# Reordering VectorE within a period of fused attention: reciprocal and output copy

## The chip, the cores and the metric

One core of one Trainium2 chip. The metric is the device time of one execution in microseconds (us); the median of several runs counts.

## The reference

Attention with a learned position bias, then two dense two-layer networks one after the other, all in float32.

```python
scores = scale * np.matmul(q, k.transpose(0, 1, 3, 2))      # B, H, S, D = 4, 8, 576, 64
...
scores = scores + bias.transpose(2, 0, 1)[None, :, :, :]
scores = scores - np.max(scores, axis=-1, keepdims=True)
attn = np.exp(scores)
attn = attn / (np.sum(attn, axis=-1, keepdims=True) + 1e-09)
x = np.matmul(attn, v)             # to (2304, 512)
h = x @ w_in;  x = (h - np.tanh(h)) @ w_out                 # d_ff = 2048
h = x @ w_in2; r = np.maximum(h, 0); x = (s * r * r + b) @ w_out2
```

The bias is a small network over log distances, computed once.

## The kernel before

The kernel has three stages: the bias table, attention, and the dense layers. Every engine carries out its instructions in the order in which the program issues them; the order is written out by hand (`manual_schedule`), and nothing rearranges it. Semaphores between engines follow from the tiles.

Attention is a software pipeline over 80 periods: 16 pairs (two heads of one batch entry) times 5 row tiles t. Tiles 0 to 3 hold 128 rows for each of two heads, so two score tiles (j = 0, 1); tile 4 holds the last 64 rows of both heads in one score tile. A row tile x = n passes through the engines over several turns n of the loop `for n in range(NK + 6)`:

- turn x: TensorE computes scores into `s` (`emit_score`, L382; two buffers); VectorE adds the bias, once for each j, and finds the extreme of each row (`emit_bias`, L389).
- turn x + 1: ScalarE takes the exponential with row sums (`emit_exp`, L403), GpSimd adds a small constant to the sums (`emit_sum`, L407), VectorE inverts them (`emit_inverse`, L411).
- turn x + 2: GpSimd scales the rows into `pn` (`emit_norm`, L420).
- turn x + 3: TensorE transposes `pn` into two banks `t0` and `t1` (`emit_transpose`, L426), and sometimes short tails into `c`; ScalarE copies `t0`, VectorE copies `t1` into `pt` (`emit_parts`, L464, or L466 and L467 for tile 4). Each of these banks exists once.
- later turns: products with v into the bank `o` (`emit_pv`, L481). A pair has two units, u = 0 with 256 rows (tiles 0 and 1) and u = 1 with 320 rows (tiles 2 to 4). Unit 0 of pair i is multiplied in turns 5i + 5 to 5i + 7, unit 1 in turns 5i + 8 and 5i + 9. `o` exists once. When a unit is complete, VectorE copies it into `xo` and SP stores that to memory (`emit_out`, L488 and L489).

So VectorE's queue in one turn n holds: bias additions of n (two, or one for tile 4), the reciprocal of n - 1, the copy of `t1` for n - 3, in two of five turns the output copy, and in every fourth turn from 15 on a tick of the weights (`weights_tick`). A tick turns packed weights into float32 with three VectorE instructions (L130, L139, L142), two on ScalarE (L122, L138) and a subtraction on GpSimd (L87). TensorE's queue in a turn: scores of n, transposes of n - 3, products. GpSimd's: scaling of n - 2, sums of n - 1, then the subtraction of a tick. SP issues in program order the loads of q and k (`load_qk`, L158), of v (L164), of bias tiles (`load_bias`, L177, inside `emit_bias`), of weights (`fetch`, L111), and the stores of `xo`.

The dense layers follow (`gemm1` L312, `gemm2` L569); TensorE works through them without the attention's buffers, and the first products of the first layer are already issued in the last turns of attention.

Of the kernel before, what the change touches and what calls it, by code (L numbers as in the profile page):

```python
# [58 lines left out]
def tile_kernel(ctx, tc, qk, vd, wcat, wts, sb, ltab, psib, ipsi8, out):  # L59
# [110 lines left out]
    def load_bias(hp, k):  # L170
        e, t = ORDER[k]
        if (hp, k) not in bias_t:
            bias_t[hp, k] = bp.tile([128, S], F32, tag="bias", name="bias")
        bt = bias_t[hp, k]
        i0, n = IT[t]
        for r, ee in enumerate((e,) if e < 2 else (0, 1)):
            nc.sync.dma_start(out=bt[r * 64:r * 64 + n], in_=bass.AP(  # L177
                tensor=bias_d.tensor, offset=bias_d.offset + i0 // 4 * (32 * PITCH - 4) + 4 * (2 * hp + ee) * PITCH + 15,
                ap=[[32 * PITCH - 4, n // 4], [PITCH - 1, 4], [1, S]]))
# [156 lines left out]
    with ExitStack() as ca:  # L336
# [30 lines left out]
        def heads_of(x):  # L367

            t = periods[x][1]
            return [(0, 8, 2)] if t == 4 else [(0, 2 * t, 0), (1, 2 * t + 1, 1)]  # L370

        def emit_score(x):
            i, t = periods[x]
            q, kk = qk_t[i]
            for j, _, e in heads_of(x):
                s = s_t[x, j] = ps_s.tile([128, 2, 512], F32, tag="s", name="s")
                for ee in ((e,) if e < 2 else (0, 1)):
                    o = s if e < 2 else s[ee * 64:ee * 64 + 64]
                    n = IT[t][1]
                    for c in range(2):  # L380
                        h = slice(c * 64, c * 64 + 64)
                        nc.tensor.matmul(o[0:n, c, 0:288], q[h, ee, t * 128:t * 128 + n], kk[h, ee], start=True, stop=True)  # L382

        def emit_bias(x):
            i, t = periods[x]
            for j, k, _ in heads_of(x):
                raw = sp.tile([128, S], F32, tag="raw", name="raw", bufs=3)
                mn = sp.tile([128, 1], F32, tag="mn", name="mn", bufs=3)
                nc.vector.tensor_tensor_reduce(  # L389
                    out=raw.rearrange("p (c j) -> p c j", c=2), in0=s_t.pop((x, j))[:, :, 0:288],  # L390
                    in1=bias_t[pairs[i][0], k].rearrange("p (c j) -> p c j", c=2),
                    scale=-0.125, scalar=3.0e38, op0=ALU.add, op1=ALU.min, accum_out=mn)
                raw_t[x, j] = (raw, mn)

                if i >= 2 and bq and 36 - len(bq) < 11 + i // B * 9 + (max(0, k + 1) if i % B == B - 1 else 0):
                    load_bias(*bq.pop(0))

        def emit_exp(x):
            sm = sums[x] = sp.tile([128, 2], F32, tag="sm", name="sm", bufs=4)
            for j, _, _ in heads_of(x):  # L400
                raw, mn = raw_t.pop((x, j))
                p = p_t[x, j] = pp.tile([128, S], F32, tag="p", name="p")
                nc.scalar.activation(out=p, in_=raw, func=AF.Exp, scale=-1.0, bias=mn, accum_out=sm[:, j:j + 1])  # L403

        def emit_sum(x):
            sm = sums[x][:, 0:len(heads_of(x))]
            nc.gpsimd.tensor_scalar(out=sm, in0=sm, scalar1=1.0, scalar2=1e-9, op0=ALU.mult, op1=ALU.add)  # L407

        def emit_inverse(x):
            sm = sums[x][:, 0:len(heads_of(x))]  # L410
            nc.vector.reciprocal(sm, sm)  # L411

        def emit_norm(x):

            pn = n_t[x] = np_.tile([128, 9 * 128], F32, tag="pn", name="pn")
            sm = sums.pop(x)
            for j, _, e in heads_of(x):
                p = p_t.pop((x, j))
                for a, b, c in ([(0, S, 0), (448, 512, S)], [(0, S, 0)], [(0, 512, 640), (512, S, S)])[(e + 1) % 3]:
                    nc.gpsimd.tensor_scalar(out=pn[:, c:c + b - a], in0=p[:, a:b], scalar1=sm[:, j:j + 1],  # L420
                                            scalar2=0.0, op0=ALU.mult, op1=ALU.add)
# [12 lines left out]
        def emit_transpose(x):  # L434
            i, t = periods[x]
            if t in (1, 3):
                emit_tails(0, x - 1)
            pn = n_t[x]
            ab = tr_t[x] = [ps_t.tile([128, 8, 64], F32, tag=f"t{r}", name=f"t{r}") for r in range(2)]
            for j in range(8 if t < 4 else 5):  # L440
                for r in range(2):
                    if t < 4:
                        c = j * 128 + j // 4 * 128
                    else:
                        c = j * 128 if j < 4 else (512, 448)[r]
                    turned(r, ab[r][:, j], pn[ROWS[r], c:c + 128])
            if t in (2, 4):
                emit_tails(1, x - 2)
                del n_t[x - 2], n_t[x - 1]
            if t == 4:  # L450
                del n_t[x]

        def emit_parts(x):

            i, t = periods[x]
            u = int(t > 1)
            if (i, u) not in unit_t:
                unit_t[i, u] = gp_.tile([128, 9, 320], F32, tag="pt", name="pt")
            pt = unit_t[i, u]
            ab = tr_t.pop(x)  # L460
            for r, copy in ((0, nc.scalar.copy), (1, nc.vector.tensor_copy)):
                if t < 4:
                    c0 = t % 2 * 128 + r * 64
                    copy(pt[:, 0:8, c0:c0 + 64], ab[r])  # L464
                else:
                    copy(pt[:, 4 * r:4 * r + 4, 256:320], ab[r][:, 0:4])  # L466
                    copy(pt[ROWS[r], 8, 256:320], ab[r][ROWS[r], 4])  # L467
            if t in (2, 4):
                done = unit_t[i, int(t == 4)]
                nc.scalar.copy(done[:, 8, 0:256], tr_t.pop("c").rearrange("p k r q -> p (k r q)"))  # L470

        def emit_pv(i, u, j):

            r0, n = UNITS[u]
            v = v_t[i]
            if j == 0:
                o_t[i, u] = ps_o.tile([128, 512], F32, tag="o", name="o")[:, 0:n]
            o = o_t[i, u]
            for e in range(2):
                h = slice(e * 64, e * 64 + 64)  # L480
                nc.tensor.matmul(o[h], v[:, e, j], unit_t[i, u][:, 8 if j == 4 else 4 * e + j, 0:n], start=(j == 0), stop=(j == 4))  # L481

        def emit_out(i, u):
            hp, b = pairs[i]
            r0, n = UNITS[u]
            del unit_t[i, u]
            xo = sp.tile([128, 320], F32, tag="xo", name="xo", bufs=2)[:, 0:n]
            nc.vector.tensor_copy(xo, o_t.pop((i, u)))  # L488
            nc.sync.dma_start(out=x1_d[hp][:, b * S + r0:b * S + r0 + n], in_=xo)  # L489

        PV = {}
        for i in range(len(pairs)):
            for u, (m, parts) in enumerate(((5 * i + 5, (2, 2, 1)), (5 * i + 8, (2, 3)))):
                js = list(range(5))
                for c, k in enumerate(parts):
                    PV.setdefault(m + c, []).append((i, u, js[:k]))
                    js = js[k:]  # L500
        for n in range(NK + 6):
            def now(lag):
                return 0 <= n - lag < NK

            if n == NK:
                s_ctx.close()
                hpool.append(h_ctx.enter_context(tc.tile_pool(name="ps_h", bufs=4, space=PSUM, side="right", reuse_waits="tile")))
            if now(2):
                emit_norm(n - 2)
            if now(0):  # L510
                emit_score(n)
            if now(1):
                emit_exp(n - 1)
                emit_sum(n - 1)
            if now(0):
                emit_bias(n)
            if now(1):
                emit_inverse(n - 1)
            if now(3):
                emit_transpose(n - 3)  # L520
                emit_parts(n - 3)
            for i, u, js in PV.pop(n, []):
                for j in js:
                    emit_pv(i, u, j)
                if js[-1] == 4:
                    emit_out(i, u)
            if n in FT:
                fetch(FT[n])
            for f in work.pop(n, []):
                f()  # L530
            for _ in range(TICKS.get(n, 0)):
                weights_tick()
            for f in PRE.get(n, []):
                f()
        assert not PV
        assert not work
# [143 lines left out]
```

## Time and profile before

| | |
|---|---|
| median of three runs | 1091.99 us (1091.46 to 1092.54) |
| the profiled execution | 1091.09 us |
| its span, first to last instruction | 1089.3 us |
| TensorE, matrix products | 1065.3 us busy (98%) |
| VectorE | 642.6 us (59%) |
| ScalarE | 469.6 us (43%) |
| GpSimd | 327.5 us (30%) |
| mean granted TensorE clock | 0.998 |

A busy share is a mean over stages with different limits. In the profile PE is TensorE, PEld its weight loads, DVE is VectorE, ACT ScalarE, POOL GpSimd, SP the queue that issues most transfers. Matrix products are pipelined, so the ends in their records are modelled.

### The profile page before, as it was taken

What the parts mean: (1) busy time and instruction counts of PE and PEld (TensorE: products, weight loads), DVE (VectorE), ACT (ScalarE), POOL (GpSimd) and SP (SyncE); (2) the same over time, 40 slices, a digit from 0 to 9 for tenths busy, and PEclk for the clock granted to TensorE, in tenths of its full rate; (3) what the DMA queues carried; (4) which work ended last, traced back from release to release, by engine and by line L of the source; (5) the groups of instructions that cost most, each with busy time, mean ns of one, the idle gap of its engine ahead of it and who ended that gap; (6) DMA issues with size and microseconds to landing.
All of it is one profiled execution on the core that took longest, in us unless ns stands there. A gap on an engine that the chain in (4) does not pass through costs nothing.

```text
span 1089.3 us, 18185 instructions
## 1 busy us (share of the span) xinstructions
PE 1065.3 (98%) x7000; PEld 838.0 (77%) x7000; DVE 642.6 (59%) x1223; ACT 469.6 (43%) x955; POOL 327.5 (30%) x454
## 2 busy tenths in 40 slices
PE   9999999999999999999999999999999999999998
PEld 6566555555678888899888888888888888888897
DVE  8878889778679832232322499997343343343344
ACT  8977677677545422222222354553222222222222
POOL 0066777678625510020300046344030030010000
PEclk9999999999999999999999999999999999999999
DMA  7957555253181010020100365500100020010010
GB/s 283 314 191 257 189 180 183 85 180 113 42 318 65 10 59 1 0 79 1 58 1 1 135 218 206 193 1 20 58 20 1 4 75 1 1 58 1 1 39 20
DMA packets 41334, 99.65 MB, mean 91 GB/s; under 512 B 5024, under 2 KB 11552, under 8 KB 41248
## 3 DMA queue, kind: packets, MB, share of 16 engines
q1 hardware_dynamic: 40960, 98.24, 26.1%
q8 instruction: 55, 0.90, 0.3%
q10 hardware_dynamic: 288, 0.26, 0.1%
q14 instruction: 31, 0.25, 0.1%
HBM read 73.41 MB, written 25.07 MB: 90 GB/s over the span
## 4 chain that ended last, share of the span: by engine, by line
PE 83%; POOL 4%; DVE 3%; DMA 2%; issue 2%; ACT 1%; ACTq 0%; SPq 0%; DVEq 0%; POOLq 0%
PE h L312 36%; PE a L569 36%; PE o L481 5%; PE s L382 4%; POOL pn L420 3%; PE t L426 2%; DMA qk<-in_qk 1%; DVE raw L389 1%; POOL w L87 1%; DVE pt L464 1%; DMA vv<-in_vd 1%; PE c L426 0%; POOL sm L407 0%; DVE wx L142 0%; DVE wx L130 0%
## 5 line engine op out<-in xcount | busy, mean ns | idle before, releaser
L312 PE MATMUL h<-x,w 128*128 128x512 f32 (+1 forms) x1920 | 420.6, 368 | 0.0
L312 PEld LDWEIGHTS h<-x,w 128*128 128x128 f32 x1920 | 337.4, 188 | 62.4 <-issue 1.3
L569 PE MATMUL a<-ring,w 128*128 128x512 f32 (+1 forms) x960 | 210.2, 368 | 0.0
L569 PE MATMUL a<-w,ring 128*128 128x512 f32 x864 | 208.9, 389 | 0.0
L569 PEld LDWEIGHTS a<-ring,w 128*128 128x128 f32 x960 | 168.3, 189 | 30.0
L569 PEld LDWEIGHTS a<-w,ring 128*128 128x128 f32 x864 | 161.1, 188 | 32.8
L87 POOL TENSOR_TENSOR w<-wx,w 128x512 fp32r<-128x512 f32 x64 | 96.0, 1500 | 209.7 <-ACT w L122 196.4
L333 DVE TENSOR_TENSOR ring<-ring 128x512 fp32r<-128x512 f32 (+1 forms) x160 | 110.3, 690 | 78.5 <-ACT ring L332 78.5
L332 ACT CAST ring<-ring 128x512 fp32r<-128x512 f32 (+1 forms) x160 | 92.3, 577 | 135.7 <-DVE ring L327 96.6
L420 POOL TENSOR_SCALAR pn<-p,sm 128x576 f32<-128x576 f32 (+2 forms) x224 | 136.8, 627 | 36.1 <-DVE sm L411 30.5
L326 DVE TENSOR_TENSOR ring<-ring 128x512 f32<-128x512 f32 (+1 forms) x80 | 53.0, 662 | 149.9 <-ACT ring L325 149.9
L323 DVE TENSOR_TENSOR ring<-h,ring 128x512 f32<-128x512 f32 (+1 forms) x80 | 50.8, 635 | 141.0 <-ACT ring L322 140.7
L84 POOL TENSOR_SCALAR x<-xr 128x512 fp32r<-128x512 f32 (+1 forms) x36 | 25.9, 719 | 330.1 <-DMA xr<-x_d 330.1
L403 ACT ACTIVATE p<-raw,mn 128x576 f32<-128x576 f32 x144 | 110.7, 773 | 13.8 <-DVE mn L389 13.0
L325 ACT ACTIVATE ring<-h 128x512 f32<-128x512 f32 (+1 forms) x80 | 44.4, 555 | 165.7 <-PE h L312 165.7
L322 ACT ACTIVATE ring<-h 128x512 f32<-128x512 f32 (+1 forms) x80 | 44.3, 554 | 164.6 <-PE h L312 164.6
L389 DVE CUSTOM_DVE_ANT_0 raw<-s,bias 128x576 f32<-128x576 f32 x144 | 103.7, 752 | 18.5 <-PE s L382 14.6
L382 PE MATMUL s<-qk 64*128 64x288 f32 (+1 forms) x640 | 93.8, 433 | 11.5 <-DVE mn L389 11.1
L481 PE MATMUL o<-pt,vv 128*64 128x256 f32 (+1 forms) x640 | 96.0, 422 | 0.0
L382 PEld LDWEIGHTS s<-qk 64*128 64x128 f32 (+1 forms) x640 | 46.3, 175 | 55.7 <-DVE mn L389 24.4
L426 PEld LDWEIGHTS t<-ident,pn 64*128 64x128 f32 x1184 | 52.5, 140 | 16.8 <-DVE pt L464 6.0
L122 ACT CAST w<-wx 128x512 fp32r<-128x512 f32 x64 | 39.7, 621 | 58.8 <-DVE wx L142 57.7
(49 smaller groups left out, 841.0 us busy)
## 6 DMA issues: line engine op xcount, KB each, us to landing
w<-in_wts SPq DMA_DIRECT2D x64, 512.0 KB, 4.7
qk<-in_qk SPq DMA_DIRECT2D x16, 864.0 KB, 6.6
bias_d<-m SPq DMA_DIRECT2D x36, 296.0 KB, 4.4
bias<-bias_d SPq DMA_DIRECT2D x32, 288.0 KB, 4.7
xr<-x_d SPq DMA_DIRECT2D x28, 256.0 KB, 3.0
vv<-in_vd SPq DMA_DIRECT2D x16, 320.0 KB, 4.2
x_d<-o SPq DMA_DIRECT2D x16, 256.0 KB, 2.1
out_x<-o SPq DMA_DIRECT2D x16, 256.0 KB, 2.1
```

The lines of the kernel that those rows point to most:

```text
L87: nc.gpsimd.tensor_tensor(out=lo, in0=raw, in1=hi.bitcast(F32), op=ALU.subtract)
L312: nc.tensor.matmul(h, a, x, start=(k == 0), stop=(k == 3 * KD - 1))
L326: nc.vector.tensor_tensor(out=g, in0=t, in1=t, op=ALU.mult)
L332: nc.scalar.copy(gh, g)
L333: nc.vector.tensor_tensor(out=gl, in0=g, in1=gh.bitcast(F32), op=ALU.subtract)
L382: nc.tensor.matmul(o[0:n, c, 0:288], q[h, ee, t * 128:t * 128 + n], kk[h, ee], start=True, stop=True)
L389: nc.vector.tensor_tensor_reduce(out=raw.rearrange("p (c j) -> p c j", c=2), in0=s_t.pop((x, j))[:, :, 0:288], in1=bias_t[pairs[i][0], k]. ...
L403: nc.scalar.activation(out=p, in_=raw, func=AF.Exp, scale=-1.0, bias=mn, accum_out=sm[:, j:j + 1])
L420: nc.gpsimd.tensor_scalar(out=pn[:, c:c + b - a], in0=p[:, a:b], scalar1=sm[:, j:j + 1], scalar2=0.0, op0=ALU.mult, op1=ALU.add)
L426: nc.tensor.transpose(out_, in_, ident[ROWS[r], ROWS[r]])
L481: nc.tensor.matmul(o[h], v[:, e, j], unit_t[i, u][:, 8 if j == 4 else 4 * e + j, 0:n], start=(j == 0), stop=(j == 4))
L569: nc.tensor.matmul(o, x, y, start=first and j == 0, stop=last and j == 2)
```

## The change

In a turn, the reciprocal of n - 1 is issued behind the copy of the transposed bank instead of in front of it. An output copy that became due in a turn is put on a list, and is issued in the next turn by `emit_bias`, in front of its last bias addition (so between the two additions of a turn with two). Its store moves along with it. From turn 79 on the output copies are issued at the end of their own turn, as before.

```diff
         def emit_bias(x):
             i, t = periods[x]
             for j, k, _ in heads_of(x):
+                if j == len(heads_of(x)) - 1:
+                    emit_outs()
                 raw = sp.tile([128, S], F32, tag="raw", name="raw", bufs=3)
...
+        outs = []
+
+        def emit_outs():
+            while outs:
+                emit_out(*outs.pop())
+
...
             if now(0):
                 emit_bias(n)
-            if now(1):
-                emit_inverse(n - 1)
             if now(3):
                 emit_transpose(n - 3)
                 emit_parts(n - 3)
+            if now(1):
+                emit_inverse(n - 1)
             for i, u, js in PV.pop(n, []):
                 for j in js:
                     emit_pv(i, u, j)
                 if js[-1] == 4:
-                    emit_out(i, u)
+                    outs.append((i, u))
+            if not now(-1):
+                emit_outs()
```

## Rows read from the trace of the kernel before

**Rows 1.** Busy time by stretch: start:end, length, busy (instructions) by engine, granted clock, DMA.

```profile
340.00:366.00 26.00, 26.00 (x117) 21.52 (x116) 26.00 (x30) 12.68 (x24) 18.46 (x14) 1.00 0.07 21
...
192.00:195.00 3.00, 2.82 (x23) 1.81 (x25) 1.55 (x5) 1.88 (x5) 2.55 (x6) 0.50 0.00 0
```

**Rows 2.** Waits, 48 to 300 us: who waited for whom, total us, times, longest.

```profile
DVE sm L411 <- POOL sm L407: 18.5, 30, 1.6
...
PE t L426 <- DVE pt L464: 3.7, 8, 1.0
...
PE t L426 <- DVE pt L467: 2.5, 5, 0.9
```

**Rows 3.** Timeline, TensorE then VectorE, an undisturbed turn: start, us, engine, line, operation.

```profile
72.09 1.24 PE L382 MATMUL s<-qk 64*128 64x288 f32 x8
...
73.88 1.08 PE L481 MATMUL o<-pt,vv 128*64 128x256 f32 x8
...
72.21 0.49 DVE L488 COPY xo<-o 128x320 f32<-128x320 f32 x1 [0.66 <-PE o L481]
72.90 0.76 DVE L389 CUSTOM_DVE_ANT_0 raw<-s,bias 128x576 f32<-128x576 f32 x1 [0.20 <-PE s L382]
```

**Rows 4.** Timeline, TensorE then VectorE, a tick behind a 256-wide unit.

```profile
122.94 1.24 PE L382 MATMUL s<-qk 64*128 64x288 f32 x8
...
124.61 1.30 PE L481 MATMUL o<-pt,vv 128*64 128x320 f32 x8
127.64 0.72 PE L382 MATMUL s<-qk 64*64 64x288 f32 x8 [1.73 <-DVE mn L389]
...
129.62 1.84 PE L481 MATMUL o<-pt,vv 128*64 128x320 f32 x12
...
123.67 0.42 DVE L488 COPY xo<-o 128x256 f32<-128x256 f32 x1
...
126.83 0.74 DVE L389 CUSTOM_DVE_ANT_0 raw<-s,bias 128x576 f32<-128x576 f32 x1
```

**Rows 5.** Timeline, TensorE then VectorE, a tick behind a 320-wide unit.

```profile
164.35 1.08 PE L481 MATMUL o<-pt,vv 128*64 128x256 f32 x8
166.04 1.43 PE L382 MATMUL s<-qk 64*128 64x288 f32 x8 [0.61 <-DVE mn L389]
...
161.47 0.17 DVE L411 RECIPROCAL sm<-sm 128x2 f32<-128x2 f32 x1 [0.53 <-POOL sm L407]
...
163.09 0.83 DVE L130 SCALAR_TENSOR_TENSOR wx<-wx,wsg 128x512 int32<-128x512 int32 x1
...
165.24 0.74 DVE L389 CUSTOM_DVE_ANT_0 raw<-s,bias 128x576 f32<-128x576 f32 x1
```

**Rows 6.** Timeline of VectorE, a tick in the turn after a 320-wide unit.

```profile
150.35 0.68 DVE L130 SCALAR_TENSOR_TENSOR wx<-wx,wsg 128x512 int32<-128x512 int32 x1
150.95 1.51 DVE L139 TENSOR_SCALAR wsg<-w 128x512 int32<-128x512 int32 x1
...
152.98 0.75 DVE L389 CUSTOM_DVE_ANT_0 raw<-s,bias 128x576 f32<-128x576 f32 x1
```

**Rows 7.** Timeline, TensorE then VectorE, a turn in which TensorE waits for a bank copy.

```profile
142.50 0.68 PE L426 MATMUL t<-ident,pn 64*128 64x64 f32 x15 [0.46 <-DVE pt L467]
143.12 1.30 PE L481 MATMUL o<-pt,vv 128*64 128x320 f32 x8
...
141.71 0.40 DVE L466 COPY pt<-t 128x256 f32<-128x256 f32 x1
```

**Rows 8.** Timeline of TensorE, the first turns of attention.

```profile
57.23 0.71 PE L426 MATMUL t<-ident,pn 64*128 64x64 f32 x15 [0.97 <-DVE pt L464]
...
59.26 0.71 PE L426 MATMUL t<-ident,pn 64*128 64x64 f32 x15 [0.30 <-DVE pt L464]
```

**Rows 9.** Timeline of TensorE, the products after a wait that ends at 190.84 us.

```profile
190.84 0.72 PE L382 MATMUL s<-qk 64*64 64x288 f32 x8 [1.73 <-DVE mn L389]
...
193.23 2.83 PE L481 MATMUL o<-pt,vv 128*64 128x320 f32 x12
```

## The prediction

> **What bounds the kernel now.** I read the stretches first [rows 1]: between 340 and 366 us, in the two dense layers, TensorE has no gap, and that lasts from about 291 us to the end. So whatever the attention stage (48 to 291 us) loses or gains arrives whole at the end, and only TensorE's position at the end of attention counts. In attention it has gaps, 1.73 us at one place [rows 4]. There every fourth period carries a piece of weight unpacking (a "tick": three VectorE instructions, 2.2 to 2.8 us).
>
> The table of waits comes next [rows 2]. VectorE stands 18.5 us, in 30 places, in front of the reciprocal (its sum comes from GpSimd). Behind it in VectorE's queue stands the copy of the transposed bank, and for that copy TensorE waits 3.7 and 2.5 us. These 6.2 us are what the first half of the change can reach. No row of TensorE waiting for an output copy is in that table: today each one is done before TensorE comes back to its bank.
>
> Last the timeline around the output copies, to see how narrow that is. In an undisturbed period [rows 3] scores start at 72.09, the first bias addition at 72.90 (0.81 behind them), and the first product of the next unit at 73.88 (1.79 behind them). The output copy runs at 72.21, before the addition, in time in which VectorE waits for scores anyway.
>
> **The change part by part.** *Reciprocal behind the copy.* No instruction more or less. Where the sum is ready, the copy starts 0.08 earlier (consecutive VectorE instructions overlap by 0.08, [rows 6]: 0.68 long, next start 0.60 later) and the reciprocal about 0.6 later. Behind the reciprocal waits the normalisation on GpSimd; its tile is transposed two periods later, so I put this at nothing: the two periods of other TensorE work hide it. If that cover were gone it would cost up to 0.6 in a period. Where the sum is late, the copy no longer waits, and TensorE gains what it waited.
>
> *Output copy between the additions.* The copies in front of the last periods stay put; 29 of 32 move, with their DMA issues. On SP's queue the DMA now follows the next period's first bias load and the q/k, v and weight fetches of its own period: these go earlier, the store goes later, and its first reader comes periods later. Nothing. On VectorE the copy (0.42 or 0.49) leaves idle time and stands in front of the second addition; score and exponent have that much slack in an undisturbed period. On TensorE it is different. There is one o bank. The next unit's first product, at the end of the same period, must wait for the copy; the copy must wait for the first addition, and that for this period's scores. Counted from the start of the scores: addition at 0.81, 0.68 for it, the copy 0.49, 0.07 to TensorE ([rows 4]: the addition at 126.83 ends at 127.57, the score starts at 127.64). That is 2.05, where TensorE is ready at 1.79 [rows 3]: 0.26 late. For the 256-wide unit, 0.81 + 0.68 + 0.42 + 0.07 = 1.98 against 1.67 ([rows 4], 122.94 to 124.61): 0.31 late. TensorE is in order, so the next scores are late too.
>
> The Trainium skill (Perfetto Trace Analysis, Matmuls) advises rotating product groups through banks, so that emptying one overlaps filling the next, and so speaks against moving this copy back with one bank. The trace of before shows no such wait, the copy coming in time; by the rule it would be exposed, which gives the places below, and without it their price is that of the first rival.
>
> The 29 places, as estimates from the same views:
>
> - Undisturbed: six at 0.26 and four at 0.31, 2.8 us.
> - A tick behind the end of a 256-wide unit (two, [rows 4]). Today copy, tick, addition; TensorE does its products at 124.61 and waits 1.73 for the addition. Then the tick starts at 123.67 and, 2.82 long (126.83 less 123.67 and 0.34), ends at 126.49; the addition takes 0.68, the copy ends at 127.59, the products start at 127.66, three us late, and the next scores 1.22 behind (1.30 less the overlap), at about 128.9 against 127.64. The wait on the bank copy behind them (about 0.5 from start to start) falls away: 0.7 each, 1.4 us.
> - A tick in the period that now holds the copy (three, [rows 6]). The copy adds 0.41 to a queue TensorE already waits for: 1.2 us.
> - A tick behind a 320-wide unit (two, [rows 5]). VectorE no longer waits for sum (0.53) or products: bank copy from 160.94 (0.59 to the next start), reciprocal (0.08), tick from 161.60. The tick took 2.15 there (163.09 to 165.24), 2.63 where it follows the bank copy directly [rows 6]. I take 2.63, being the order that it will have: addition at 164.23, output copy to 165.40, products at 165.47, next scores at about 166.49 against 166.04: 0.45 each, 0.9 us. With 2.15 it would be nothing.
> - Where TensorE waits on a bank copy today (twelve places with their neighbours, [rows 7] is one). There the copies start at 141.18 instead of 141.71, the addition at 141.85, the output copy ends at 142.95, the products start at 143.02 against 143.12. The wait goes, but lateness of the output copy takes all but 0.1 of it. So four times -0.1, twice -0.2 for a pair of places where a tick has made VectorE late, twice +0.1, and -0.2 and -0.4 at single places: -1.2 us.
> - The start [rows 8]: no output copy yet, and TensorE waits 0.97 and 0.30 for bank copies. Of these 1.27 I take back 1.1; normalisation then limits.
>
> On the tick behind a 320-wide unit, the three instructions would run beside GpSimd's subtraction of the same weights, and the sign extraction there took 1.51 [rows 6], more than the two other instructions of that tick together. The Trainium skill (SBUF — State Buffer, Who interferes with whom) says VectorE and GpSimd share a port pair as an exclusive lock, and the later one blocks for the whole instruction. By that rule the tick is the long one (the sum as above); without it 0.9 less. The trace agrees, with 1.51.
>
> Sum: 2.8 + 1.4 + 1.2 + 0.9 - 1.2 - 1.1 = +4.0 us. The profiled execution took 1091.09 (span 1089.3 and 1.8 around it), so 1095.1 in its terms; it lies 0.9 below the median of the runs, 1091.99, so 1096.0 as a median.
>
> **Rivals.** *Only the swap is felt (faster).* If TensorE's products are not really ready when their records start (starts are of pipelined instructions), the output copy stays hidden. This decides if the copy arrives 0.31 earlier relative to them. Then the 6.2 us of waits come back, less 1.2 for the three ticks: 1091.99 - 5.0 = 1087.0. For it: the records' ends are modelled. Against: additions and products are measured on the same starts, and the distances repeat from unit to unit. Chance 0.14.
>
> *Cancelled (no change).* If the copy is late by only half, 0.14 less at 29 places, 4.0 goes: 1092.0. Chance 0.20, with all mixtures near it.
>
> *Clock (slower still).* TensorE idles 1.73 twice, before 127.64 [rows 4] and before 190.84 [rows 9]. After the second the granted clock stood at 0.50, the level of 1.2 GHz, from 192 to 195 us [rows 1], and the same twelve products took 2.83 [rows 9] against 1.84 after the first [rows 4]; with the transposes in front I put it at 1.4. With the change it idles for three us before 127.66 and likewise a turn later. If it falls after both, +1.4: 1097.4; if after neither, 1094.6. The first I give 0.22, inside "slower".
>
> That the order isn't carried out can't be: queues are in written order here.
>
> **How the numbers follow.** Forecast alone 0.44, clock 0.22, so slower 0.66; cancelled 0.20; swap alone 0.14. A measurement can tell about 0.2% (2.2 us) from no change. The likeliest is 1096.0. Below, half the lateness gives 1092, and a bit of it the start; above, the clock (1.4) and normalisation, if it loses its cover in a few periods (0.6 each), give 1098 to 1099. The range 1091.0 to 1099.0 leaves out the swap alone and little else. The forecast's own range is 1093 to 1098.
>
> **What would show it.** In the waits a new row, TensorE's products waiting for the output copy, in most of 29 places, 0.2 to 0.4 each and three us at two ticks; the row of TensorE's transposes waiting for bank copies close to gone; the waits before the reciprocal shorter than 18.5. Five undisturbed periods should take 0.57 more. Scores of the first dense product should start some 4 us later. Wrong would be: no such row of products, or waits of the transposes on normalisation, or an end of attention that comes earlier.

## The result and the profile after

The changed kernel takes 1100.63 us (median of four runs, 1097.51 to 1101.96) against 1091.84 (four runs, 1091.46 to 1092.54): the ratio is 1.0076, 95% interval 1.0053 to 1.0098. It is slower, as forecast, but by 8.8 us and not by 4, and lies above the range. The profiled execution took 1101.96; the head of its page, span and busy times:

```profile
span 1099.9 us, 18176 instructions
...
PE 1066.9 (97%) x7000; PEld 840.0 (76%) x7000; DVE 643.6 (59%) x1223; ACT 469.8 (43%) x955; POOL 328.6 (30%) x454
```

Each engine is busy within 1.6 us of before, so of the 10.6 us by which the span grew most is in the gaps. The first product of the first dense layer starts at 301.95 us, against 291.33: the whole loss is there by then, as the prediction's first reading of the trace had it.

The waits of the attention stage, 48 to 310 us, columns as in [rows 2]; first a line of the kernel before, then the changed kernel:

```profile
POOL pn L420 <- DVE sm L411: 30.5, 51, 2.4
```

```profile
POOL pn L422 <- DVE sm L413: 47.7, 50, 2.9
...
PE o L483 <- DVE xo L490: 13.4, 16, 3.0
...
DVE sm L413 <- POOL sm L409: 3.9, 8, 1.0
...
PE s L382 <- DMA qk<-in_qk: 1.3, 1, 1.3
```

Half of this is what the swap was to do: VectorE stands 3.9 us in front of the reciprocal and no longer 18.5, and no row of transposes waiting for a bank copy is left. The other half is the new row in the middle: TensorE's products wait for the output copy, 13.4 us in 16 places, up to 3.0 us. The table of before has no such row. The timeline shows more than these 16: at each of the 29 moved copies the first product of the next unit starts 0.10 to 0.15 behind the copy's end. The normalisation (`pn`) waits 47.7 us for the later reciprocal, against 30.5 before; the prediction priced that at nothing. The last row is a wait of the scores for a load of q and k, at turn 20; it comes up again below.

A quiet place, TensorE and then VectorE: the first product of a unit behind an output copy.

```profile
65.05 1.24 PE L382 MATMUL s<-qk 64*128 64x288 f32 x8
66.13 0.66 PE L428 MATMUL t<-ident,pn 64*128 64x64 f32 x16
67.17 1.30 PE L483 MATMUL o<-pt,vv 128*64 128x320 f32 x8 [0.38 <-DVE xo L490]
```

```profile
65.47 0.23 DVE L469 COPY pt<-t 64x64 f32<-64x64 f32 x1
65.72 0.17 DVE L413 RECIPROCAL sm<-sm 128x2 f32<-128x2 f32 x1
65.92 0.76 DVE L391 CUSTOM_DVE_ANT_0 raw<-s,bias 128x576 f32<-128x576 f32 x1
...
66.61 0.42 DVE L490 COPY xo<-o 128x256 f32<-128x256 f32 x1
```

The transposes are done at 66.79. The output copy stands behind the first addition, starts at 66.61 and ends at 67.03; the product starts at 67.17, 0.14 behind that end.

The place of [rows 4], the tick behind a 256-wide unit, TensorE and VectorE:

```profile
126.38 0.66 PE L428 MATMUL t<-ident,pn 64*128 64x64 f32 x16
130.03 2.40 PE L483 MATMUL o<-pt,vv 128*64 128x320 f32 x8 [2.98 <-DVE xo L490]
...
134.78 2.45 PE L483 MATMUL o<-pt,vv 128*64 128x320 f32 x12
```

```profile
126.06 0.67 DVE L130 SCALAR_TENSOR_TENSOR wx<-wx,wsg 128x512 int32<-128x512 int32 x1
126.65 1.50 DVE L139 TENSOR_SCALAR wsg<-w 128x512 int32<-128x512 int32 x1
...
128.78 0.76 DVE L391 CUSTOM_DVE_ANT_0 raw<-s,bias 128x576 f32<-128x576 f32 x1
...
129.46 0.42 DVE L490 COPY xo<-o 128x256 f32<-128x256 f32 x1
```

TensorE stands 2.98 us, as worked out ("three us late"). But the products that follow take 2.40 where the same eight took 1.30 [rows 4], and the twelve 2.45 against 1.84. The windows tell why (columns as in [rows 1], the clock is the number 1.00 or 0.5 behind the last bracket):

```profile
126.00:129.00 3.00, 1.04 (x22) 0.76 (x18) 2.97 (x5) 2.53 (x6) 2.96 (x2) 1.00 0.00 0
129.00:136.00 7.00, 5.97 (x40) 2.93 (x42) 3.76 (x11) 2.85 (x6) 3.47 (x9) 0.52 0.53 169
136.00:139.00 3.00, 3.00 (x36) 1.90 (x32) 1.03 (x3) 0.31 (x3) 1.75 (x4) 0.99 0.00 0
198.00:204.00 6.00, 5.84 (x38) 2.84 (x40) 2.89 (x9) 2.50 (x6) 2.47 (x8) 0.50 0.06 22
```

The granted clock is at half, the level of 1.2 GHz, from 129.25 to 136.08 us: it falls while TensorE stands, 0.8 us before the products start. In the second such stand it falls at 197.52, with products at 198.16, and is back at 204.34. Each stretch is 6.83 us long. Before, the profiled execution had one stretch at half, of 3.41 us [rows 1].

### The profile page after: what moved, and what is told of

Its sections match the earlier page's. It is cut to its first block, busy times and chain, and to the rows that moved or that the text cites. A ratio compares the mean times of both kernels' runs of the same rounds, so it can differ in the third digit from the quotient of the medians.

```text
span 1099.9 us, 18176 instructions
## 1 busy us (share of the span) xinstructions
PE 1066.9 (97%) x7000; PEld 840.0 (76%) x7000; DVE 643.6 (59%) x1223; ACT 469.8 (43%) x955; POOL 328.6 (30%) x454
## 4 chain that ended last, share of the span: by engine, by line
PE 90%; DVE 4%; DMA 2%; issue 2%; POOL 1%; ACT 0%; SPq 0%; ACTq 0%; DVEq 0%
PE h L312 36%; PE a L579 36%; PE o L483 7%; PE s L382 5%; PE b L259 3%; PE t L428 2%; DVE raw L391 2%; DMA qk<-in_qk 1%; PE c L428 1%; DVE xo L490 1%; POOL pn L422 0%; DVE wx L142 0%; DMA bias_d<-m 0%; DMA bias<-bias_d 0%; DVE hid L240 0%
## 5 line engine op out<-in xcount | busy, mean ns | idle before, releaser
L422 POOL TENSOR_SCALAR pn<-p,sm 128x576 f32<-128x576 f32 (+2 forms) x224 | 136.0, 623 | 54.4 <-DVE sm L413 47.7
L483 PE MATMUL o<-pt,vv 128*64 128x256 f32 (+1 forms) x640 | 98.6, 429 | 18.1 <-DVE xo L490 13.4
L483 PEld LDWEIGHTS o<-pt,vv 128*64 128x64 f32 x640 | 42.6, 140 | 41.7 <-issue 11.3
L139 DVE TENSOR_SCALAR wsg<-w 128x512 int32<-128x512 int32 x64 | 62.8, 982 | 4.9 <-DMA w<-in_wts 4.9
```

Of the source, the lines that this page charges most:

```text
L139: nc.vector.tensor_scalar(out=sg, in0=hw, scalar1=-2 ** 31, scalar2=1, op0=ALU.bitwise_and, op1=ALU.bitwise_or)
```

## The experiments

All times are medians with the ratio to the kernel before, run on the same chip beside it. The four runs of the changed kernel had a mean granted clock of 0.993 to 0.998, those of the kernel before, in all pairings, 0.995 to 1.0; where the order alone is meant, executions in which it stayed at 1.0 are compared. For the kernel before, five of these lie at 1088.91 to 1089.52, and with extra transposes (below) at 1088.68 to 1089.32: about 1089.2.

**Each half alone.** The swap alone, with the output copies where they were:

```diff
-            if now(1):
-                emit_inverse(n - 1)
             if now(3):
                 emit_transpose(n - 3)
                 emit_parts(n - 3)
+            if now(1):
+                emit_inverse(n - 1)
```

> Only the reciprocal behind the bank copy; output copies where they were. If the output copies are what costs (one o bank), this gains part of the 6.2 us of waits for bank copies: 1087 to 1090, and the row of transposes waiting for bank copies nearly gone. If the reciprocal, 0.6 us later, costs through a late normalisation on GpSimd, it is 1096 or more and transposes wait for the normalisation.

The outputs alone are the changed kernel with these lines back in front.

> Only the output copies behind the first addition; the reciprocal in front of the bank copy as before. If the output copies cost, 1098 to 1104, with products waiting for the output copy in most of 29 places and about three us at two. If the swap costs, near 1092.

The swap alone: 1085.04 us (1082.95 to 1086.15), ratio 0.9931 (0.9916 to 0.9946). The outputs alone: 1104.04 (1103.40 to 1104.27), 1.0105 (1.0086 to 1.0124). The waits of the swap alone, then of the outputs alone:

```profile
DVE sm L411 <- POOL sm L407: 13.2, 21, 1.5
...
PE t L426 <- DVE pt L464: 0.5, 2, 0.2
...
PE o L481 <- DVE xo L488: 0.2, 1, 0.2
```

```profile
PE o L483 <- DVE xo L490: 11.0, 15, 3.0
...
DVE sm L413 <- POOL sm L409: 8.7, 17, 1.2
...
PE t L428 <- DVE pt L466: 2.1, 4, 1.0
```

The swap does what it was to do, and gains more than was expected of it: TensorE's waits on the big bank copy go from 3.7 to 0.5 us, and the row of 2.5 us for the two-piece copy is gone. In executions at clock 1.0 it gains 5.8 us (1083.4, the mean of two, against 1089.2). All loss belongs to the output copies. Behind them the swap is still worth something, 1104.04 to 1100.63 or 3.4 us, but less than half of the 7.8 that it gains alone, and the products' wait for the output copy grows from 11.0 to 13.4.

**The output copy in front of the first addition** instead of the last:

```diff
-                if j == len(heads_of(x)) - 1:
+                if j == 0:
                     emit_outs()
```

> The changed kernel, but the output copy is issued in front of the first bias addition of the next turn, not the last. VectorE's order is then that of the swap alone, except that a tick comes in front of the copy. If the loss comes from standing behind the first addition, the undisturbed places lose nothing any more and it is 1087 to 1092, with two to three us of waiting and a clock drop left at turns 28 and 48. If already the move past the end of the turn costs, 1097 or more.

1086.00 us (1083.72 to 1088.72), 0.9944 (0.9931 to 0.9956), a little below what was expected: 14.6 us below the changed kernel, clock losses included, by a copy that stands one place earlier in its queue. The wait of products for the output copy:

```profile
PE o L483 <- DVE xo L490: 7.6, 4, 2.2
```

It is left in four places only. Against the swap alone (1085.04, on another chip) to take the copy into the next turn costs about 1 us, which lies within the spread of the runs; the rest comes from its place behind the first addition, which itself waits for the scores of the same turn.

**Two banks for `o`.** All banks were in use, so the short tails were transposed into the two large banks instead of `c`, in this run and in a control that has the same tails and one `o` bank (`bufs=1`). What is copied for the last 64 keys is then not their tails; both kernels leave these out. The edit, cut:

```diff
-        ps_o = ca.enter_context(tc.tile_pool(name="ps_o", bufs=1, space=PSUM, reuse_waits="tile"))
+        ps_o = ca.enter_context(tc.tile_pool(name="ps_o", bufs=2, space=PSUM, reuse_waits="tile"))
...
-        def emit_tails(r, x):
-            if r == 0:
-                tr_t["c"] = ps_t.tile([128, 2, 2, 64], F32, tag="c", name="c")
+        def emit_tails(r, x, t0):
             for k in range(2):
-                turned(r, tr_t["c"][:, k, r], n_t[x + k][ROWS[r], 512:640])
+                turned(r, t0[:, k], n_t[x + k][ROWS[r], 512:640])
...
-                nc.scalar.copy(done[:, 8, 0:256], tr_t.pop("c").rearrange("p k r q -> p (k r q)"))
+                nc.scalar.copy(done[:, 8, 0:256], ab[0][:, 0:4].rearrange("p k q -> p (k q)"))
```

> The changed order with two banks for the products in place of one. To free a bank the transposed tails (the last 64 keys) go into the banks of the other transposes and what is copied for them is not the tails, so the output is wrong in those keys; the instructions are as many and as large. If the single bank is what makes the copy's place costly, no product waits for an output copy, no clock drop beyond that of before, and it is 1085 to 1091. If the cost comes from the delayed second addition, it is as its control with one bank.

> Control for the two banks: the same rerouted tails (wrong in the last 64 keys), one bank for the products. 1099 to 1104, as the changed kernel, a little more where the tails now wait for the bank of the transposes.

Two banks: 1088.43 us (1085.89 to 1088.98), 0.9958 (0.9945 to 0.9971). The control: 1098.37 (1097.53 to 1101.14), 1.0059 (1.0047 to 1.0071), just under what was expected. The products' wait for the output copy in the control:

```profile
PE o L481 <- DVE xo L488: 13.5, 16, 3.0
```

The run with two banks has no such row. The second bank is worth 9.9 us, clock losses included. That is more than the 8.8 us that the change lost: with two banks this order is no slower than the kernel before.

**The copy in front of the tick**, in the turns that end with one:

```diff
-            if not now(-1):
+            if not now(-1) or n in TICKS:
                 emit_outs()
```

> The changed kernel, but in turns with a tick the output copy is issued at the end of its own turn, in front of the tick (turns 19, 27, 39, 47, 59, 74). If the two waits of three us and the clock behind them make the part that the prediction missed, 1093 to 1096, granted clock 0.998 or more, and the runs lie closer together than 1097.5 to 1102.0. If the missing part is spread over all 29 places, 1098 to 1099.

1095.88 us (1093.90 to 1097.78), 1.0029 (1.0016 to 1.0043), 4.8 below the changed kernel. The wait goes from 13.4 to 8.5 us, the longest is now 1.5:

```profile
PE o L483 <- DVE xo L490: 8.5, 14, 1.5
```

Two of its eight runs stayed at clock 1.0, with 1094.03 and 1093.90; the four at 0.998 lie at 1095.67 to 1096.85 (two more lie at 0.997). The profiled one of these (1095.67) had one stretch of 3.41 us at half; by these runs such a stretch costs some 1.7 to 2.9 us, 1.9 at the median.

**TensorE kept busy in the two stands.** In turns 28 and 48 the transposes are issued four times, into the stand. This adds work and takes none away (from here on, the busy version):

```diff
-        def emit_transpose(x):
+        def emit_transpose(x, times=1):
...
-            for j in range(8 if t < 4 else 5):
+            for j in [*range(8 if t < 4 else 5)] * times:
...
-                emit_transpose(n - 3)
+                emit_transpose(n - 3, 4 if n in (28, 48) else 1)
```

> The changed kernel, but in turns 28 and 48 the transposes are issued four times over into the same banks, some 2.1 us of extra TensorE work in the three us in which it stands. The order and every wait stay. If the clock fell because TensorE stood still, it stays at 1.0 there, and the time falls in spite of more work, to 1094 to 1097. If the place costs by the wait alone, or the clock falls anyway, 1100 to 1102.

1096.57 us (1096.04 to 1097.51), 1.0040 (1.0027 to 1.0053): 4.1 faster than the changed kernel, with more to do. TensorE's timeline and the windows there:

```profile
125.71 2.16 PE L428 MATMUL t<-ident,pn 64*128 64x64 f32 x64
129.37 1.30 PE L483 MATMUL o<-pt,vv 128*64 128x320 f32 x8 [1.50 <-DVE xo L490]
```

```profile
124.00:127.00 3.00, 3.00 (x56) 2.32 (x56) 2.96 (x9) 2.98 (x8) 2.38 (x4) 1.00 0.04 16
127.00:134.00 7.00, 5.50 (x76) 3.21 (x74) 5.07 (x13) 4.05 (x10) 5.58 (x11) 1.00 0.49 159
193.00:200.00 7.00, 5.51 (x63) 3.12 (x60) 4.51 (x12) 3.67 (x8) 5.58 (x11) 1.00 0.06 19
```

The clock stays at 1.00 behind both places, and the same products take 1.30 again. The products still wait for the output copy, so the stands' loss of clock is separate from the wait itself, and this run shows the changed order without it: 1096.4, the middle of this run and its repetition below.

The same extra transposes (three times) with the order of before and with the swap alone:

> The kernel before, with the same extra transposes in turns 28 and 48. If its runs differ by whether and how long the clock falls, all of them now lie together at 1088.5 to 1090.5 with a granted clock of 1.0. It is the level from which the changed kernel with its standing filled (1096.6) is then to be counted: by the sum of the prediction 4 us of difference, by the periods of that trace nearer 6 to 7.

> The swap alone, with the transposes of turns 28 and 48 issued three times over (1.4 us of extra TensorE work each, in front of 1.7 us in which it stands). If the clock falls there because TensorE stands, it now stays at 1.0 in every run: 1083.0 to 1084.0, the level of those runs of the swap alone that had no drop. If the extra work costs as much, 1085 or more.

With the order of before: 1091.89 (1088.68 to 1094.70), 1.0001 (0.9988 to 1.0014). The expectation missed: three of twelve runs stayed at 1.0, in the others the clock fell all the same. Where it fell in those is not known, as the trace that was kept is of a run at 1.0. With the swap alone: 1083.91 (1083.62 to 1084.70), 0.9925 (0.9913 to 0.9937), every run at 0.999 or 1.0. That is the fastest version found, 8.7 us below the kernel before beside it (1092.62); against the swap without the trick (1085.04), run on another chip, it is within the spread of that one's runs.

**The short piece of the bank copy first**, in the turns that copy a tile 4 (L468, L469), on top of the busy version, with a repetition of that version beside it:

```diff
-                    copy(pt[:, 4 * r:4 * r + 4, 256:320], ab[r][:, 0:4])
                     copy(pt[ROWS[r], 8, 256:320], ab[r][ROWS[r], 4])
+                    copy(pt[:, 4 * r:4 * r + 4, 256:320], ab[r][:, 0:4])
```

> The kernel with filled standing in turns 28 and 48 (so without clock drops there), and where the bank copy is two pieces, the short piece from partition 64 is issued first. In the changed kernel 0.03 us pass on each side of the reciprocal behind the short piece and it overlaps with nothing, so that the first addition starts some 0.13 later than the prediction had it. If the short piece is the reason, additions behind it start 0.1 earlier in 15 turns and the time falls by 1 to 2 us against the same kernel without this edit (1096.6). If not, no difference.

> The kernel with filled standing once more, as the level for the run beside it: 1096 to 1097.5, granted clock 1.0 or 0.999 in every run.

Short piece first: 1095.21 (1094.81 to 1095.88), 1.0032 (1.0021 to 1.0043). Repetition: 1096.17 (1095.47 to 1096.42), 1.0037 (1.0023 to 1.0050). VectorE in one such turn, the repetition and then the short piece first:

```profile
64.43 0.42 DVE L468 COPY pt<-t 128x256 f32<-128x256 f32 x1
64.87 0.23 DVE L469 COPY pt<-t 64x64 f32<-64x64 f32 x1
65.12 0.17 DVE L413 RECIPROCAL sm<-sm 128x2 f32<-128x2 f32 x1
65.32 0.76 DVE L391 CUSTOM_DVE_ANT_0 raw<-s,bias 128x576 f32<-128x576 f32 x1
```

```profile
64.84 0.23 DVE L468 COPY pt<-t 64x64 f32<-64x64 f32 x1
65.08 0.42 DVE L469 COPY pt<-t 128x256 f32<-128x256 f32 x1
65.42 0.16 DVE L413 RECIPROCAL sm<-sm 128x2 f32<-128x2 f32 x1
65.55 0.76 DVE L391 CUSTOM_DVE_ANT_0 raw<-s,bias 128x576 f32<-128x576 f32 x1
```

Behind the short piece, which lies in partitions 64 to 127, the reciprocal starts 0.02 after its end; behind a full copy it starts 0.08 before. The medians differ by 1.0 us, about the lower end of what was expected, and 15 such turns at 0.07 (0.89 against 0.82 from the end of the second addition to the next turn's first) would be 1.05. The Trainium skill (VectorE: DVE Perf Modes, "Two Vector instructions with no wait between them") says that an instruction whose access starts in another quadrant of partitions than the last one is held until the earlier ones have finished. The trace agrees: a gap of 0.02 instead of an overlap of 0.08.

**The reciprocal back in front of the copy, in four turns.** The last two runs ask what made the term that was furthest off; both are the busy version with this edit:

```diff
+            if n in (36, 57, 62, 72):          # the second run: (36, 56, 61, 71)
+                emit_inverse(n - 1)
             if now(3):
                 emit_transpose(n - 3, 4 if n in (28, 48) else 1)
                 emit_parts(n - 3)
-            if now(1):
+            if now(1) and n not in (36, 57, 62, 72):
                 emit_inverse(n - 1)
```

> The changed order with the extra transposes of turns 28 and 48 (1096.2 to 1096.6 us, clock at 1.0), but in turns 36, 57, 62 and 72 the reciprocal stands in front of the bank copy again. Theory: the later reciprocal lets the normalisation on GpSimd begin 0.6 us later, the next sum stands behind it in GpSimd's queue, and the next reciprocal, now directly in front of the first bias addition, waits 0.26 to 0.28 for that sum in turns 37, 58, 63 and 73. Then the waits of turns 37, 58 and 73 go, the additions behind them come some 0.2 us earlier each (0.26 less 0.08 for the reciprocal in front of the copy), and the first dense product comes 0.4 to 0.8 us earlier; in turn 62 the normalisation started 1.0 us behind its reciprocal, so there nothing should change. Median some 0.6 below, near 1095.8, which the medians hardly tell and the trace does. Rival: the normalisation is held by something else (the exponentials, GpSimd's other work), the waits stay, each of the four places loses 0.08 or nothing, and the median is 1096.2 to 1096.9.

1097.46 us (1096.76 to 1098.33), 1.0053 (1.0039 to 1.0067). The list was one turn off at three places: there the reciprocal that waits was itself put in front. Taken against the repetition of the busy version, the first addition behind turn 37 comes 0.22 earlier, those behind turns 57 and 72 come 0.57 later each. Turn 62 can't be read, as its wait differs between the two runs of the busy version (0.27 and 0.58).

> As the run before it, with the reciprocal in front of the bank copy in turns 36, 56, 61 and 71, each the turn before one in which the reciprocal waits 0.26 to 0.28 us for its sum and holds the next first bias addition. (In the run before, turns 57, 62 and 72 were those of the waiting reciprocal itself: only turn 36 was placed as meant, and there the next additions came 0.21 earlier; turns 57 and 72 cost 0.58 and 0.57.) Theory: the late normalisation, caused by the moved reciprocal of the turn before, is what makes the sum late. Then the additions behind turns 37 and 57 come 0.21 earlier each, as that one did, and behind 72 some 0.2, if GpSimd's other work (0.62 before that normalisation) leaves it room; at 62 nothing changes, the normalisation there being behind a subtraction of GpSimd's own (1.3 us). In all some 0.6 earlier at turn 79 than the same order without it, apart from the start; median near 1095.6. Rival: only the first place has this cause, the waits behind 57 and 72 stay, and the sum is 0.2.

1095.48 us (1094.91 to 1096.25), 1.0041 (1.0028 to 1.0055). Around turn 37, GpSimd and VectorE in the repetition of the busy version, then in this run:

```profile
158.56 1.71 POOL L422 TENSOR_SCALAR pn<-p,sm 128x576 f32<-128x576 f32 x3 [1.10 <-PE s L382]
160.35 0.19 POOL L409 TENSOR_SCALAR sm<-sm 128x2 f32<-128x2 f32 x1
```

```profile
158.25 0.15 DVE L413 RECIPROCAL sm<-sm 128x2 f32<-128x2 f32 x1
...
160.58 0.17 DVE L413 RECIPROCAL sm<-sm 128x2 f32<-128x2 f32 x1 [0.27 <-POOL sm L409]
160.77 0.76 DVE L391 CUSTOM_DVE_ANT_0 raw<-s,bias 128x576 f32<-128x576 f32 x1
```

```profile
157.37 1.72 POOL L422 TENSOR_SCALAR pn<-p,sm 128x576 f32<-128x576 f32 x3 [0.49 <-PE s L382]
159.17 0.19 POOL L409 TENSOR_SCALAR sm<-sm 128x2 f32<-128x2 f32 x1
```

```profile
157.05 0.15 DVE L413 RECIPROCAL sm<-sm 128x2 f32<-128x2 f32 x1
...
159.75 0.17 DVE L413 RECIPROCAL sm<-sm 128x2 f32<-128x2 f32 x1
159.94 0.76 DVE L391 CUSTOM_DVE_ANT_0 raw<-s,bias 128x576 f32<-128x576 f32 x1
```

In the first, the reciprocal of the turn before ends at 158.40, the normalisation starts at 158.56, the next sum stands behind it on GpSimd, and the next reciprocal waits 0.27 for that sum, right in front of an addition. (The table puts the normalisation's wait down to TensorE's scores; that its start follows the reciprocal here too is what the edit shows.) With that one reciprocal moved forward, the wait is gone. Against the repetition, the first additions come 0.22, 0.22 and 0.23 earlier behind turns 37, 57 and 72: 0.67 us, about what was expected. At turn 62 the reciprocal still waits 0.31; its sum stands behind a subtraction of GpSimd's own.

The rest of the difference at the end of attention, 0.9 us, arises at turn 20, before the first of these turns, and is none of this edit. TensorE's scores there, in the repetition and then in this run:

```profile
101.87 1.24 PE L382 MATMUL s<-qk 64*128 64x288 f32 x8 [1.11 <-DMA qk<-in_qk]
```

```profile
101.15 1.24 PE L382 MATMUL s<-qk 64*128 64x288 f32 x8
```

The scores of a new pair wait for its q and k, or don't. The load is issued at 93.2 to 93.9 us in all of these profiles; it landed 8.3 to 8.6 us later in the changed kernel and in the three other runs that have its order up to there (the two busy versions and the run before this one), 7.3 later in this run, which has that order too, and 6.3 and 7.3 later in the two profiles of the order of before.

## Why the prediction was right or wrong

The first additions of all 80 periods, in the busy version less the order of before at clock 1.0 with the extra transposes (the profiled executions of 1096.04 and 1089.32 us), give the loss by place. The sum of the prediction against it:

| term | predicted | measured |
|---|---|---|
| the start | -1.1 | -1.3 |
| undisturbed, copy of a 320-wide unit (six) | 1.6 | 1.7 |
| undisturbed, copy of a 256-wide unit (four) | 1.2 | 2.0 |
| tick behind a 256-wide unit (two) | 1.4 | 1.4 |
| tick in the copy's own period (three) | 1.2 | 1.2 |
| tick behind a 320-wide unit (two) | 0.9 | 0.3 |
| twelve places with a wait on a bank copy | -1.2 | +2.1 |
| sum | +4.0 | +7.4 |
| clock, after less before | 0 | +1.6 |

The last line is in medians: 1100.6 - 1096.4 = 4.2 us for the changed kernel less 1091.8 - 1089.2 = 2.6 for the kernel before. It and the sum together are the 8.8 us of the result, but for 0.2.

**Right.** The mechanism: one `o` bank, a copy that waits for an addition that waits for this period's scores, and a product at the period's end that waits for the copy. The new row of waits, the bank copies' row gone, the shorter wait of the reciprocal, three us at two ticks, and a loss that arrives whole at the dense layers are all in the trace. The two-bank run with its control and the move in front of the first addition show the cause. Of the three terms in which a tick decides, two came out to a tenth of a microsecond. The Trainium skill's advice (Perfetto Trace Analysis, Matmuls) to rotate product groups through banks agrees with the runs here: 9.9 us for a second bank. "Cancelled" and "only the swap is felt" fell; the second's price was fair all the same, since the swap alone gains 5.8 us at clock 1.0, where 6.2 of waits were counted.

**The step that failed most** is the term "Where TensorE waits on a bank copy today", twelve places at -1.2. It was said that the wait goes, "but lateness of the output copy takes all but 0.1 of it". The places lost 2.1 together, 3.3 more than forecast. Most went at turn 20 (0.75), at 38 and 58 (0.55 each) and at 63 (0.39); turns 33, 53 and 68 lost about 0.1 each, and the others together gained some 0.45.

Part of it is the step before, "reciprocal about 0.6 later ... I put this at nothing: the two periods of other TensorE work hide it". The cover was looked for on the wrong engine. TensorE's work hides the normalisation's own tile, but GpSimd is in order too: behind the late normalisation stands the next sum, behind that the next reciprocal, and this one now stands directly in front of the next first addition. Shown at three places, 0.67 us together.

Another part is a second step that was put at nothing, the transfers ("Nothing" for SP's queue). At turn 20 the busy version waits for q and k; in the run whose load landed in time, with the same order up to there, the same place gained 0.15 where it had lost 0.75. So 0.9 of the 3.3 is a late load and not the place of the output copy. Whether the new order of the transfers made it late, or it varies by itself, is not shown. The remaining 1.7 or so is located, not taken apart: at 38 and 58 some 0.33 is left, the price of an undisturbed place, as if the wait on the bank copy that went had given back nothing, and at 63 the wait varies between two runs of the same kernel.

**Mis-sized.** The undisturbed places behind a 256-wide unit cost 0.45 at three and 0.65 at one, and not 0.31: the bank copy in front comes in two pieces there, and the reciprocal and addition behind the short one start without overlap (short piece first: 1.0 us less), and from the copy's end to the product 0.14 passes where 0.07 was taken. These two make the 0.45; what the 0.65 has more is not taken apart. The tick behind a 320-wide unit did take the 2.63 assumed (in the busy version it starts at 165.39 and the addition at 168.00), but its place lost 0.15 and not 0.45; why is open.

**The clock** was seen as a risk at the right two places, with +1.4 "if it falls after both", but the sum itself went without it. In the profiled execution it fell at both, for 6.83 us each time and not 3.41 [rows 1]. From turn 26 to turn 31 the profiled kernels lie 3.7 us further apart, of which the order alone explains 1.0; one such stretch costs 2.7, more than was priced. To keep TensorE at work there brought 4.1 us back. In the medians the clock made only 1.6 of the difference, near the 1.4, because the kernel before loses 2.6 to its clock as well: that the two nearly agree is luck. The failed term (3.3 more than forecast) and the clock (1.6) together carry the time out of the range.

## What to carry to other kernels

When a copy empties the only bank that the next product group fills, look at what the copy stands behind in its engine's queue: an instruction that waits for work of the same period of the product engine makes a loop through both queues, and its length, start to start, is the price at every unit. When an instruction is moved later "under cover", follow the queue of each engine that reads it, not only its data: the next thing in that queue is late as well. Long stands of TensorE are to be priced twice, as the stand and as what its clock does afterwards. And a load that lands just in time can turn a place of the sum by itself: compare several profiles before its loss is put down to the order.

## What was not expected of the hardware

The granted clock went to half for twice as long as in the trace of before, 6.83 against 3.41 us, each time in a stand of about 3 us. That length is not fixed: the control of the two banks, whose longest wait for the copy is 3.0 us as well, had one stretch of 3.41 in its profiled execution, from 129.89 to 133.30. The clock was kept up by transposes whose results are simply written again (2.16 us of transposes in one stand, where there were 0.66). In the order of before the same filling, three times and not four, did not help: the clock fell in nine of twelve runs; where and why is open.
